# Attention values with the attention weights stationary, row sums from a ones column, and the result turned by the DMA crossbar

## Chip, cores, metric

One core of a Trainium2 chip. The metric is the time of one execution in device microseconds. The kernel before takes 1127.8 us (median of 4 runs, 1127.23 to 1130.22).

## The reference, cut to what matters

```python
def _attn_ref(q, kv, w_sr):            # q: 4 x 12288 x 128, kv: 4 x 384 x 32 x 128
    kv_pool = kv.reshape(B, H // 4, 4, W // 4, 4, C).mean(axis=(2, 4))
    k = v = kv_pool.reshape(B, -1, C) @ w_sr           # 768 keys of 128
    s = (q @ k.transpose(0, 2, 1)) / np.sqrt(C)
    a = softmax(s)                                      # rows of 768
    return a @ v

def _moe_ref(x, w_gate, w_val, w_out):                  # x: the 49152 attention rows; d_ff 1536
    return (np.maximum(x @ w_gate, 0) * (x @ w_val)) @ w_out
```

The kernel leaves the softmax unnormalised through the feed-forward part. Because that part is of degree two in x, one multiplication by the squared reciprocal of the row sum, at the very end, sets it right.

## The kernel before

A tile is 512 tokens, a group is four tiles, and there are 96 tiles. Tile k passes through a software pipeline: scores and exp in iteration k, values in k+1, value and gate projections in k+3, output projection in k+4. Cuts are marked with `# ...`.

```python
    def scores(k, jc):                       # TensorE, then exp on ScalarE
        s_ps = bank([128, T])
        nc.tensor.matmul(s_ps, kv16[:, k // NST, jc, 0, :], qT_of(k), start=True, stop=True)
        nc.scalar.activation(aTs[k][:, jc, :], s_ps, AF.Exp, scale=qk_scale)

    def values(k, jc):                       # kv stationary, 512 columns of weights stream
        # ...
        nc.tensor.matmul(xt_banks[k], kv16[:, k // NST, jc, 1, :], aTs[k][:, jc, :],
                         start=(jc == 0), stop=(jc == NJC - 1))
        if jc == NJC - 1:
            xTs[k] = work.tile([128, T], FP16, tag="xT", bufs=7, name="xT")
            nc.vector.tensor_copy(xTs[k], xt_banks.pop(k))       # already the way the next step wants it

    def row_sums(g):                         # once a group: 24 matmuls with a block of ones
        # ...
    def row_norms(g):                        # once a group: four fp32 transposes, reciprocal, square
        # ...

    def project(b, jc, pooled, copy_a, copy_b):       # pooled kv -> k and v
        tp = bank([128, 128])
        # ... transpose into tp
        kvT = work.tile([128, 128], FP32, tag="kvT")
        copy_a(kvT, tp)
        pr = bank([128, 2, 128])
        nc.tensor.matmul(pr[:, 0, :], w_sr_f32, kvT, start=True, stop=True)
        nc.tensor.matmul(pr[:, 1, :], kvT, w_sr_f32, start=True, stop=True)
        copy_b(kv16[:, b, jc], pr)
    # ... in the loop over k = 3 .. 98, for step in range(12):
    #     out_proj(k-4, step); value_proj(k-3, step); scores(k) or values(k-1); gate_proj(k-3, step)
    #     for each of batches 1 to 3, six times, in the batch before: kv_load (SyncE) at step 1,
    #     pooling on GpSimd at step 3 two tiles later, project at step 7 two tiles after that
```

The softmax here doesn't subtract the row's maximum and nothing guards it: scores larger than these inputs give would overflow.

## Time and profile before

| | before |
|---|---|
| time, median | 1127.8 us |
| span of the profiled run | 1125.7 us |
| TensorE, VectorE, ScalarE busy | 96%, 82%, 81% |
| one tile in the loop without inserts | 10.445 us |
| inserts per group (row sums, their turn) | 1.50 + 0.44 us |
| a tile with a kv projection (18 of them) | 11.27 us |

The rows on a tile and on inserts are distances from start to start. The lines are in the prediction.

### The profile page before, as it was taken

What the parts mean: (1) busy time and instruction counts of PE and PEld (TensorE: products, weight loads), DVE (VectorE), ACT (ScalarE), POOL (GpSimd) and SP (SyncE); (2) the same over time, 40 slices, a digit from 0 to 9 for tenths busy, and PEclk for the clock granted to TensorE, in tenths of its full rate; (3) what the DMA queues carried; (4) which work ended last, traced back from release to release, by engine and by line L of the source; (5) the groups of instructions that cost most, each with busy time, mean ns of one, the idle gap of its engine ahead of it and who ended that gap; (6) DMA issues with size and microseconds to landing.
All of it is one profiled execution on the core that took longest, in us unless ns stands there. A gap on an engine that the chain in (4) does not pass through costs nothing.

```text
span 1125.7 us, 23319 instructions
## 1 busy us (share of the span) xinstructions
PE 1077.6 (96%) x8874; PEld 636.3 (57%) x8874; DVE 920.1 (82%) x1470; ACT 909.2 (81%) x1741; POOL 119.8 (11%) x124
## 2 busy tenths in 40 slices
PE   0599999999999999999999999999999999999998
PEld 0245555556555555556555555555655555555555
DVE  1278888888888888888888888888888888888888
ACT  0488788778888888887888888878888888888886
POOL 1184000333000000042000000000000000000000
PEclk9999999999999999999999999999999999999999
DMA  9999530457303303313133033031230310201001
GB/s 217 222 220 245 94 57 30 94 118 156 66 24 62 58 29 66 57 30 57 35 52 65 22 66 58 29 58 47 39 67 23 64 38 29 48 20 29 20 29 38
DMA packets 166065, 78.24 MB, mean 70 GB/s; under 512 B 104129, under 2 KB 153409, under 8 KB 165953
## 3 DMA queue, kind: packets, MB, share of 16 engines
q1 hardware_dynamic: 112848, 59.85, 22.5%
q0 software_dynamic: 51376, 13.76, 12.1%
q10 hardware_dynamic: 1728, 3.15, 1.1%
q8 instruction: 69, 1.13, 0.4%
q14 instruction: 44, 0.35, 0.1%
HBM read 52.76 MB, written 25.17 MB: 69 GB/s over the span
## 4 chain that ended last, share of the span: by engine, by line
PE 94%; DMA 3%; ACT 1%; SPq 1%; DVE 0%; issue 0%; ACTq 0%; DVEq 0%; POOLq 0%
PE bank_ps L221 23%; PE bank_ps L196 22%; PE bank_ps L207 22%; PE bank_ps L150 11%; PE bank_ps L156 11%; PE bank_ps L170 3%; DMA q<-in_q_dram 1%; PE bank_ps L133 1%; PE bank_ps L182 1%; DMA parts<-in_kv_dram 1%; SPq L84 1%; DMA out_dram<-o_sb 1%; ACT aT L151 1%; PE bank_ps L134 1%; PE bank_ps L126 0%
## 5 line engine op out<-in xcount | busy, mean ns | idle before, releaser
L210 DVE SCALAR_TENSOR_TENSOR hT<-bank_ps,val 128x512 f16<-128x512 f32 x1152 | 764.7, 687 | 133.4 <-ACT val L200 83.2
L200 ACT CAST val<-bank_ps 128x512 f16<-128x512 f32 x1152 | 676.5, 589 | 166.1 <-PE bank_ps L196 164.6
L221 PEld LDWEIGHTS <-hT 128*128 128x128 f16 x4608 | 349.7, 98 | 262.9 <-issue 10.2
L221 PE MATMUL bank_ps<-wo,hT 128*128 128x128 f16 x4608 | 441.1, 219 | 0.9 <-DVE hT L210 0.8
L196 PE MATMUL bank_ps<-xT,wv 128*128 128x512 f16 x1152 | 436.6, 379 | 0.2
L207 PE MATMUL bank_ps<-xT,wg 128*128 128x512 f16 x1152 | 436.6, 379 | 0.0
L151 ACT ACTIVATE aT<-bank_ps 128x512 f16<-128x512 f32 x576 | 344.9, 602 | 3.1 <-PE bank_ps L150 3.1
L156 PE MATMUL bank_ps<-aT,kv 128*128 128x512 f16 x576 | 216.6, 379 | 2.8 <-DVE o_sb L229 2.1
L150 PE MATMUL bank_ps<-qT,kv 128*128 128x512 f16 x576 | 216.3, 381 | 2.4 <-ACT kv L138 2.4
L207 PEld LDWEIGHTS <-wg 128*128 128x128 f16 x1152 | 112.7, 98 | 134.5 <-issue 3.6
L196 PEld LDWEIGHTS <-wv 128*128 128x128 f16 x1152 | 112.7, 98 | 4.5 <-issue 1.4
L74 POOL DMA_DIRECT2D q<-in_q_dram x24 | 27.9, 1164 | 660.3 <-DMA qT<-q 659.5
L162 DVE CAST xT<-bank_ps 128x512 f16<-128x512 f32 x96 | 65.1, 680 | 10.7 <-PE bank_ps L156 10.7
L229 DVE TENSOR_TENSOR o_sb<-bank_ps,inv 128x512 f32<-128x512 f32 x96 | 65.3, 680 | 3.2 <-DMA out_dram<-o_sb 2.7
L150 PEld LDWEIGHTS <-kv 128*128 128x128 f16 x576 | 56.0, 98 | 6.2 <-ACT kv L138 4.0
L156 PEld LDWEIGHTS <-kv 128*128 128x128 f16 x576 | 56.3, 98 | 4.5 <-issue 1.2
L110 POOL TENSOR_TENSOR s<-parts 128x512 f32<-128x512 f32 x36 | 45.7, 1285 | 7.9 <-DMA parts<-in_kv_dram 7.1
L170 PE MATMUL bank_ps<-aT,ones 128*32 128x512 f16 x576 | 35.5, 381 | 0.0
L110 DVE TENSOR_TENSOR s<-parts 128x512 f32<-128x512 f32 x12 | 8.3, 692 | 33.2 <-DMA parts<-in_kv_dram 33.2
L133 PE MATMUL bank_ps<-kvT,w_sr_f 128*128 128x128 f32 x48 | 11.3, 319 | 24.5 <-ACT kvT L131 24.0
L131 ACT ACT_TABLE_LOAD x1 | 1.3, 1283 | 36.1 <-DMA parts<-in_kv_dram 36.1
L170 PEld LDWEIGHTS <-ones 128*32 128x32 f16 x576 | 13.2, 96 | 20.4 <-issue 9.9
(28 smaller groups left out, 161.5 us busy)
## 6 DMA issues: line engine op xcount, KB each, us to landing
out_dram<-o_sb SPq DMA_DIRECT2D x96, 256.0 KB, 2.2
parts<-in_kv_dram SPq DMA_DIRECT2D x84, 256.0 KB, 7.0
q<-in_q_dram POOLq DMA_DIRECT2D x24, 512.0 KB, 6.3
parts<-in_kv_dram ACTq DMA_DIRECT2D x12, 256.0 KB, 8.7
wv<-in_moe_w_val_dram POOLq DMA_DIRECT2D x1, 384.0 KB, 19.0
wg<-in_moe_w_gate_dram POOLq DMA_DIRECT2D x1, 384.0 KB, 21.2
wo<-in_moe_w_out_dram POOLq DMA_DIRECT2D x1, 384.0 KB, 25.5
qT<-q SPq DMA_TRANSPOSE x24, 4.3
```

Source lines behind the costliest of these rows:

```text
L110: eng.tensor_tensor(s2[:, i], parts[:, 2 * i], parts[:, 2 * i + 1], op=ALU.add)
L150: nc.tensor.matmul(s_ps, kv16[:, k // NST, jc, 0, :], qT_of(k), start=True, stop=True)
L151: nc.scalar.activation(aTs[k][:, jc, :], s_ps, AF.Exp, scale=qk_scale)
L156: nc.tensor.matmul(xt_banks[k], kv16[:, k // NST, jc, 1, :], aTs[k][:, jc, :], start=(jc == 0), stop=(jc == NJC - 1),)
L162: nc.vector.tensor_copy(xTs[k], xt_banks.pop(k))
L170: nc.tensor.matmul(r_ps[32 * i : 32 * i + 32, :], ones, aTs[g * GRP + i][:, jc, :], start=(jc == 0), stop=(jc == NJC - 1),)
L196: nc.tensor.matmul(va_ps, wv16[:, fb * 128 : (fb + 1) * 128], xTs[k], start=True, stop=True)
L200: nc.scalar.copy(val, va_ps)
L207: nc.tensor.matmul(g_ps, wg16[:, fb * 128 : (fb + 1) * 128], xTs[k], start=True, stop=True)
L210: nc.vector.scalar_tensor_tensor(hTs[k][:, fb, :], g_ps, 0.0, vals.pop((k, fb)), op0=ALU.max, op1=ALU.mult)
L221: nc.tensor.matmul(o_ps[:, s, :], hTs[k][:, fb, s * 128 : (s + 1) * 128], wo16[:, fb, :], start=(fb == 0 and s == 0), stop=(fb == NFB - 1) ...
L229: nc.vector.tensor_tensor(o_sb, o_banks.pop(k), inv2.to_broadcast([128, NS, 128]), op=ALU.mult)
```

## The change

The intent is to take the row sums off TensorE. With the attention weights stationary (128 tokens at a time) and k/v streaming, a column of ones beside v gives the row sum in the same matmul. The result then has tokens on the partitions and has to be turned before the projections, which a transposing DMA does (through the crossbar of the DMA engines). A second part of the change is the order of tokens: a q load now puts 16 consecutive tokens on a partition, four for each tile of the group, and an output write four.

```diff
-            q16, q[b, n0 : n0 + GRP * T, :].rearrange("(s p) c -> p s c", p=128)
+            q16, q[b, n0 : n0 + GRP * T, :].rearrange("(p s) c -> p s c", p=128)
-    kv16 = const.tile([128, B, NJC, 2, 128], FP16)
+    kv16 = const.tile([128, B, NJC, 2 * C + 4], FP16)          # k, v, ones
-    def values(k, jc):
-        nc.tensor.matmul(xt_banks[k], kv16[:, k // NST, jc, 1, :], aTs[k][:, jc, :], ...)
+    def values(k, jc, half):
+        for i in range(2):
+            s = 2 * half + i
+            nc.tensor.matmul(
+                x_ps[:, i, :], aTs[k][:, jc, s * 128 : (s + 1) * 128],
+                kv16[:, k // NST, jc, C : 2 * C + 1], ...)       # 129 columns
         if jc == NJC - 1:
-            nc.vector.tensor_copy(xTs[k], xt_banks.pop(k))
+            nc.vector.tensor_copy(x16s[k][:, own, :], x_ps[:, :, 0:C])
+            nc.vector.reciprocal(rinvs[k][:, own], x_ps[:, :, C])
+            if half == 1:
+                nc.sync.dma_start_transpose(xT, x16.rearrange("p s c -> p (s c)"))
+                nc.vector.tensor_tensor(inv2s[k][:, :, 0], rinv, rinv, op=ALU.mult)
-    def row_sums(g): ...
-    def row_norms(g): ...
-                out[k * T : (k + 1) * T, :].rearrange("(s p) c -> p s c", p=128), o_sb
+                out[k // GRP * GRP * T : (k // GRP + 1) * GRP * T, :].rearrange(
+                    "(p i s) c -> i p s c", p=128, i=GRP)[k % GRP], o_sb
     # ... before the loop: values of tiles 0 and 1 only (four before);
     #     tiles 2 and 3 follow in iterations 3 and 4; aT has 5 buffers (6 before)
```

More of the change, by code (lines that the diff above doesn't have):

```diff
@@ L134, in project @@
         nc.tensor.matmul(pr[:, 1, :], kvT, w_sr_f32, start=True, stop=True)
-        copy_b(kv16[:, b, jc], pr)
+        copy_b(kv16[:, b, jc, 0 : 2 * C], pr.rearrange("p i c -> p (i c)"))
     def act_scaled(dst, src):
@@ L141, in dve_scaled @@
         nc.vector.tensor_scalar(dst, src, 1.0 / (r * r), None, op0=ALU.mult)
-    aTs, xt_banks, xTs, hTs, o_banks, inv2s, vals = {}, {}, {}, {}, {}, {}, {}
+    aTs, x_banks, x16s, xTs, rinvs, inv2s = {}, {}, {}, {}, {}, {}
+    hTs, o_banks, vals = {}, {}, {}
     def scores(k, jc):
         if jc == 0:
-            aTs[k] = work.tile([128, NJC, T], FP16, tag="aT", bufs=6, name="aT")
+            aTs[k] = work.tile([128, NJC, T], FP16, tag="aT", bufs=5, name="aT")
         s_ps = bank([128, T])
-        nc.tensor.matmul(s_ps, kv16[:, k // NST, jc, 0, :], qT_of(k), start=True, stop=True)
+        nc.tensor.matmul(s_ps, kv16[:, k // NST, jc, 0:C], qT_of(k), start=True, stop=True)
@@ L151, in scores @@
         nc.scalar.activation(aTs[k][:, jc, :], s_ps, AF.Exp, scale=qk_scale)
-    def values(k, jc):
+    def values(k, jc, half):
         if jc == 0:
-            xt_banks[k] = bank([128, T])
-        nc.tensor.matmul(
-            xt_banks[k], kv16[:, k // NST, jc, 1, :], aTs[k][:, jc, :],
-            start=(jc == 0), stop=(jc == NJC - 1),
-        )
-        if jc == NJC - 1:
-            xTs[k] = work.tile([128, T], FP16, tag="xT", bufs=7, name="xT")
-            nc.vector.tensor_copy(xTs[k], xt_banks.pop(k))
@@ L164 @@
-    r_state = {}
-    def row_sums(g):
-        r_ps = bank([128, T])
-        for jc in range(NJC):
-            for i in range(GRP):
-                nc.tensor.matmul(
-                    r_ps[32 * i : 32 * i + 32, :], ones, aTs[g * GRP + i][:, jc, :],
-                    start=(jc == 0), stop=(jc == NJC - 1),
-                )
-        r_sb = work.tile([128, T], FP32, tag="r_sb")
-        nc.vector.tensor_copy(r_sb, r_ps)
-        r_state[g] = r_sb
-    def row_norms(g):
-        r_sb = r_state.pop(g)
-        rT = bank([128, NS, 128])
-        for s in range(NS):
-            nc.tensor.matmul(
-                rT[:, s, :], r_sb[:, s * 128 : (s + 1) * 128], ident,
-                is_transpose=True, start=True, stop=True,
-            )
-        rinv = work.tile([128, NS, GRP], FP32, tag="rinv")
-        nc.vector.reciprocal(
-            rinv, rT.rearrange("p s (g w) -> p s g w", g=GRP)[:, :, :, 0]
-        )
-        inv2 = work.tile([128, NS, GRP], FP32, tag="inv2", bufs=3)
-        nc.vector.tensor_tensor(inv2, rinv, rinv, op=ALU.mult)
-        inv2s[g] = inv2
+            x_banks[k, half] = bank([128, 2, C + 1])
@@ new lines, in values @@
+            if half == 0:
+                x16s[k] = work.tile([128, NS, C], FP16, tag="x16", bufs=3, name="x16")
+                rinvs[k] = work.tile([128, NS], FP32, tag="rinv", bufs=3, name="rinv")
+        x_ps = x_banks[k, half]
+        for i in range(2):
+            s = 2 * half + i
+            nc.tensor.matmul(
+                x_ps[:, i, :], aTs[k][:, jc, s * 128 : (s + 1) * 128],
+                kv16[:, k // NST, jc, C : 2 * C + 1],
+                start=(jc == 0 and i == 0), stop=(jc == NJC - 1), skip_group_check=True,
+            )
@@ new lines, in values @@
+        if jc == NJC - 1:
+            own = slice(2 * half, 2 * half + 2)
+            nc.vector.tensor_copy(x16s[k][:, own, :], x_ps[:, :, 0:C])
+            nc.vector.reciprocal(rinvs[k][:, own], x_ps[:, :, C])
+            if half == 1:
+                x16 = x16s.pop(k)
+                xT = work.tile([128, NS, 128], FP16, tag="xT", bufs=6, name="xT")
+                nc.sync.dma_start_transpose(xT, x16.rearrange("p s c -> p (s c)"))
+                xTs[k] = xT.rearrange("c s p -> c (s p)")
+                rinv = rinvs.pop(k)
+                inv2s[k] = work.tile([128, NS, 1], FP32, tag="inv2", bufs=6, name="inv2")
+                nc.vector.tensor_tensor(inv2s[k][:, :, 0], rinv, rinv, op=ALU.mult)
@@ L227, in out_proj @@
             o_sb = work.tile([128, NS, 128], FP32, tag="o_sb", bufs=3)
-            inv2 = inv2s[k // GRP][:, :, k % GRP : k % GRP + 1]
             nc.vector.tensor_tensor(
-                o_sb, o_banks.pop(k), inv2.to_broadcast([128, NS, 128]), op=ALU.mult
+                o_sb, o_banks.pop(k), inv2s.pop(k).to_broadcast([128, NS, 128]), op=ALU.mult
             )
             nc.sync.dma_start(
-                out[k * T : (k + 1) * T, :].rearrange("(s p) c -> p s c", p=128), o_sb
+                out[k // GRP * GRP * T : (k // GRP + 1) * GRP * T, :].rearrange(
+                    "(p i s) c -> i p s c", p=128, i=GRP
+                )[k % GRP], o_sb,
             )
@@ L244 @@
     make_identity(nc, ident)
-    ones = const.tile([128, 32], FP16)
-    nc.gpsimd.memset(ones, 1.0)
+    nc.gpsimd.memset(kv16[:, :, :, 2 * C : 2 * C + 4], 1.0)
     q_turn(0)
@@ L262 @@
         if jc > 0:
-            for k in range(LEAD):
-                values(k, jc - 1)
+            for k in range(2):
+                for half in range(2):
+                    values(k, jc - 1, half)
         if jc == 2:
@@ L268 @@
             nc.gpsimd.dma_start(wo16, moe_w_out.rearrange("(fb f) c -> f fb c", f=128))
-    for k in range(LEAD):
-        values(k, NJC - 1)
+    for k in range(2):
+        for half in range(2):
+            values(k, NJC - 1, half)
     q_turn(1)
@@ L292 @@
                     scores(k, step // 2)
-            elif LEAD <= k - 1 < NT:
-                values(k - 1, step // 2)
+            elif 2 <= k - 1 < NT:
+                half, i = divmod(step // 2, NJC // 2)
+                values(k - 1, 2 * i, half)
+                values(k - 1, 2 * i + 1, half)
             if 0 <= kF < NT:
                 gate_proj(kF, step)
-            if ph == 0 and k >= GRP and k // GRP <= NG:
-                if step == 2:
-                    row_sums(g - 1)
-                if step == 5:
-                    row_norms(g - 1)
             if b < B:
```

## The prediction

> **What bounds the kernel now.** I read the page's busy shares and its 40 slices first.
>
> ```profile
> PE 1077.6 (96%) x8874; PEld 636.3 (57%) x8874; DVE 920.1 (82%) x1470; ACT 909.2 (81%) x1741; POOL 119.8 (11%) x124
> PE   0599999999999999999999999999999999999998
> DMA  9999530457303303313133033031230310201001
> PE 94%; DMA 3%; ACT 1%; SPq 1%; DVE 0%; issue 0%; ACTq 0%; DVEq 0%; POOLq 0%
> ```
>
> TensorE is busy from slice 3 to the end, and 94% of the chain that ended last is TensorE. A busy TensorE is not proof, because matmuls overlap, so I then read the timeline of one stretch in the middle (TensorE only; columns are start us, length, line, count).
>
> ```profile
> 605.81 0.38 PE L207 MATMUL bank_ps<-xT,wg 128*128 128x512 f16 x1
> 606.03 0.39 PE L221 MATMUL bank_ps<-wo,hT 128*128 128x128 f16 x4
> 606.25 0.38 PE L196 MATMUL bank_ps<-xT,wv 128*128 128x512 f16 x1
> 606.47 0.38 PE L150 MATMUL bank_ps<-qT,kv 128*128 128x512 f16 x1
> 606.68 0.38 PE L207 MATMUL bank_ps<-xT,wg 128*128 128x512 f16 x1
> 606.99 1.48 PE L170 MATMUL bank_ps<-aT,ones 128*32 128x512 f16 x24
> 608.40 0.40 PE L221 MATMUL bank_ps<-wo,hT 128*128 128x128 f16 x4
> ...
> 610.81 0.38 PE L207 MATMUL bank_ps<-xT,wg 128*128 128x512 f16 x1
> 611.03 0.60 PE L182 MATMUL bank_ps<-ident,r_sb 128*128 128x128 f32 x4
> 611.47 0.39 PE L221 MATMUL bank_ps<-wo,hT 128*128 128x128 f16 x4
> ```
>
> The starts, not the lengths, are to be read: a 512-column matmul takes a slot of 0.216 us, four 128-column ones (each with its own weights) take 0.22 to 0.23, and no slot is empty. In the records' nanoseconds the median start-to-start is 216 ns for all 512-column lines and 56 ns for L221. So TensorE streams without a gap. A step of the loop (out 4x56, value 216, scores or values 216, gate 216) is 0.87 us, a tile of 12 steps 10.45 us (two output copies lie at 136.83 and 147.28), a group of four tiles 43.75 us. The group is 4 x 10.445 = 41.78 plus two inserts: the row sums (L170, 606.68 + 0.216 to 608.40: 1.50 us) and their turn (L182, 611.03 to 611.47: 0.44 us).
>
> **What the Trainium skill says.** "TensorE: Matmul & The Clock Gate", section "Wait — 56ns, not 53.3ns?", gives a warm start-to-start of N/2.4 + 2.5 ns: 55.6 for 128 columns and 215.7 for 512. The trace agrees (56 and 216). The same page, "Back-to-back issue gap", expects about 81 ns for a 128-column matmul with its own weight load; here L221 runs at 56 with a fresh load for each, so the loads (98 ns long in their rows, started 56 ns apart) are hidden and the trace decides. "DMA: Bandwidth & Descriptors", section "Specifications", asks for at least 512 B per descriptor for full rate; before, the q reads and out writes are runs of 512 B, so larger runs should help, and only where DMA is short. The same page's "Issuing engines are not separate DMA queues" says that all queues share the 16 engines; the early phase below shows it.
>
> **The change, part by part.** (1) Row sums and their turn go away: 24 x (1.50 + 0.44) = 46.6 us, all of it inserted in the gapless stream, so all on the path. (2) Values: 576 matmuls of 512 columns become 2304 of 129 columns, each with its own attention weights. Slot: 129/2.4 + 2.5 = 56.2 ns (an estimate from the page above and the 56 measured for 128). 576 x (4 x 56.2 - 216) = +5.1 us. The pattern "four short ones with loads between two long ones" is exactly that of L221, so I choose to believe that the loads stay hidden. (1)+(2): -41.5 us while TensorE is the bound.
>
> (3) VectorE. Per tile now: 12 gate products, one output copy, one xT copy and a quarter of the row-sum work. What counts is the start-to-start when it catches up:
>
> ```profile
> 604.41 0.68 DVE L229 TENSOR_TENSOR o_sb<-bank_ps,inv 128x512 f32<-128x512 f32 x1
> 605.01 0.68 DVE L162 CAST xT<-bank_ps 128x512 f16<-128x512 f32 x1
> 605.61 2.47 DVE L210 SCALAR_TENSOR_TENSOR hT<-bank_ps,val 128x512 f16<-128x512 f32 x4
> 612.13 0.25 DVE L187 RECIPROCAL rinv<-bank_ps 128x16 f32<-128x16 f32 x1
> 612.41 0.17 DVE L191 TENSOR_TENSOR inv<-rinv 128x16 f32<-128x16 f32 x1
> ```
>
> A full-bank operation costs 0.60, a tiny one 0.28 to 0.31. Removed per tile: 0.60 for xT and (0.60 + 0.28 + 0.31)/4 = 0.30. Added: two 128x256 copies at about 0.33 (half of 512 elements less the fixed part; an estimate), two reciprocals at 0.28, one product at 0.31: 1.53. VectorE goes from 12 x 0.60 + 0.60 + 0.90 = 8.7 to 9.3 us a tile, below TensorE's 10.45 + 0.05 = 10.50, so it stays beside the path, at 89%. Its page share should rise from 82% to about 88%. ScalarE has the same work: 909/1092 = 83%.
>
> (4) The xT turn moves to the DMA crossbar. Transposing 512 KB of q took 2048 packets of 256 B at 18 ns, 2.3 us of 16 engines; 128 KB is 0.58 us a tile, 55 us in all, on DMA that is idle two thirds of the time. From issue to landing q's took 4.3 us at best; a quarter of it perhaps 2.5 us (estimate). In the loop, tile k's values end in iteration k+1 and xT is wanted in k+3, so one iteration of 10.5 us covers it. (5) Four consecutive tokens: q's cast loads (51,376 packets in all, 41 ns each, 5.4 us of 16 engines per load) get longer runs, as do the out writes (0.87 us each). That is off the path except early.
>
> (6) The start is where I expect to pay. Until about 112 us DMA is full (9 in the first four slices), and the SyncE queue holds back whatever stands behind the kv loads:
>
> ```profile
> 60.93 11.10 SPq L101 DMA_DIRECT2D parts<-in_kv_dram  x11
> 72.78 7.94 SPq L84 DMA_TRANSPOSE qT<-q  x1
> 80.77 23.87 SPq L101 DMA_DIRECT2D parts<-in_kv_dram  x23
> 105.35 0.42 SPq L232 DMA_DIRECT2D out_dram<-o_sb  x1
> ```
>
> The first output was ready at 80.5 us and issued at 105.35, 25 us late; a q transpose takes 8 us to issue. Before, that cost one stall of 2.5 us (at 111.8, output buffers). Now xT itself goes through this queue. xT of tile 0 is ready to turn at about 62 us, where before it was used at once (61.5). I guess it is issued between 62 and 72 and lands 4 to 8 us after: TensorE waits 6 to 18 us, with 4 us of scores and values to fill in. Later tiles have an iteration of slack, and the delay itself gives them more. The old stall of 2.5 us should shrink. Two tiles' values move from the start into the loop (2.7 us), where the first gate products bound it anyway (12 x 0.60 = 7.2 us against 24 x 0.216 = 5.2). Net: +6 us, between 0 and +18.
>
> **Sum.** 1127.4 - 46.6 + 5.1 + 6 = 1092 us.
>
> **Rivals.** A: the weight loads from aT are not hidden, or an odd 129 columns costs extra. If a pair took the page's 81 ns: 2304 x 25 = +58 us, about 1150 and slower. Against it: L221 does the same at 56. For it: odd steps would then have 8 of 10 matmuls short. I give it 5%. B: VectorE or the PSUM banks become the bound. Its burst at a tile's end grows from 1.2 (output copy and xT) to about 1.5 us, plus 0.6 in the middle of the tile, with 0.27 us a step (0.87 less 0.60) to recover. The last copy and its reciprocals hold a bank while eight are near full. A gap of 0.1 us a tile is +10 us: about 1100. Before, the burst caused no TensorE gap, hence I count it as the upper part of the range. C: the SyncE queue holds xT for its whole 25 us lag, less a few us of slack: +20, so 1106 and only just 2%. D: nothing shows at the start, because the queue's order puts the transposes early and the longer q runs relieve DMA: 1083 to 1086.
>
> **Range and chances.** D and C set the ends: 1082 to 1107. The 2% line is 1104.8; only C with B, or A, crosses it. Faster 0.87, same 0.10, slower 0.03.
>
> **What would show it.** Right: L170 and L182 gone; the values line has 2304 matmuls 56 ns apart in start; group pitch about 42.0 us (4 x 10.50) instead of 43.75; VectorE near 88%; one TensorE wait on the xT transpose of 5 to 15 us between 60 and 75 us, and hardly any wait after 115; share of q0 down. Wrong: values starting over 60 ns apart (A); regular TensorE gaps that wait on VectorE (B); TensorE waits on xT in the middle of the run, which would mean that the transposes stand behind other work in the SyncE queue or take far longer than 2.5 us.

## More of the kernel before

Medians of several runs are quoted.

What the program writes is not the order that runs. A scheduler of the framework sorts each engine's instructions, and lets the kv loads of batches 1 and 2 run ahead from about 44 us on, although the program writes the first of them in iteration 12.

One more view is needed later, a projection of kv in the timeline of the kernel before (columns: start us, length us, engine, line, operation). First TensorE, then VectorE:

```profile
220.87 0.27 PE L126 MATMUL bank_ps<-ident,s 128*128 128x128 f32 x1
220.97 0.61 PE L221 MATMUL bank_ps<-wo,hT 128*128 128x128 f16 x8
221.61 0.46 PE L133 MATMUL bank_ps<-kvT,w_sr_f 128*128 128x128 f32 x2
```

```profile
221.18 0.29 DVE L131 COPY kvT<-bank_ps 128x128 f32<-128x128 f32 x1
```

The transpose of the pooled keys (L126, the last of it here) starts at 220.87, VectorE copies kvT at 221.18, and the projection matmul follows at 221.61: eight short output matmuls lie between, and they are enough.

## The result and the profile after

The changed kernel takes 1117.41 us (median of 4 runs, 1115.73 to 1119.26): ratio 0.9904, 95% interval 0.9881 to 0.9928. Ratios are the mean time of one kernel's runs over that of the other's of the same rounds, so they are not quite the ratios of the medians quoted. The change gains 1%, within the 2% line. The prediction was 1092 us, with 1082 to 1107 as its range.

From the page of the changed kernel: busy shares, slices of TensorE and of its granted clock, the chain by engine, then groups (busy us, mean ns | idle us before them) and a DMA issue with its us to landing.

```profile
PE 1041.0 (93%) x9930; PEld 688.4 (62%) x9930; DVE 918.9 (82%) x1782; ACT 904.8 (81%) x1741; POOL 104.3 (9%) x124
PE   0538999999999999999999999999999999999998
PEclk9969999999999999999999999999999999999999
PE 87%; DMA 6%; SPq 2%; ACT 2%; DVE 2%; issue 0%; POOL 0%; POOLq 0%; DVEq 0%
L185 PE MATMUL bank_ps<-xT,wv 128*128 128x512 f16 x1152 | 437.6, 380 | 25.7 <-DMA xT<-x 25.7
L165 PE MATMUL bank_ps<-kv,aT 128*128 128x129 f16 x2304 | 224.3, 220 | 0.1
xT<-x SPq DMA_TRANSPOSE x96, 2.5
```

The row sums are gone, and the chain has lost 7 points of TensorE to DMA, its queue, ScalarE and VectorE. The third slice of TensorE is down to 3 tenths, with the clock at 6 tenths there, and the value projection L185 waited 25.7 us in four places for xT. The 129-column matmuls themselves wait for nothing (0.1 us). Nor do the smaller buffers (aT has 5, before 6) show: after 115 us TensorE has no gap over 0.1 us but those named below and one of 0.8 us at the end, which the kernel before has too. Once in the loop, output copies are 10.515 us apart (134.79, 145.31 and on), against 10.445 before.

Where the waits lie is shown by the timeline of the changed kernel around the start, TensorE, then the SyncE queue (xN counts DMA issues, the length runs to the end of the last):

```profile
57.45 0.89 PE L165 MATMUL bank_ps<-kv,aT 128*128 128x129 f16 x8
76.87 0.58 PE L185 MATMUL bank_ps<-xT,wv 128*128 128x512 f16 x1 [18.53 <-DMA xT<-x]
...
79.39 0.63 PE L196 MATMUL bank_ps<-xT,wg 128*128 128x512 f16 x1
79.82 0.63 PE L185 MATMUL bank_ps<-xT,wv 128*128 128x512 f16 x1
```

```profile
50.83 16.24 SPq L103 DMA_DIRECT2D parts<-in_kv_dram  x17
67.65 6.62 SPq L85 DMA_TRANSPOSE qT<-q  x1
74.37 2.52 SPq L177 DMA_TRANSPOSE xT<-x  x2
```

VectorE has finished x of tile 0 at 58.6 us. Its transpose is issued at 74.37: for 16 us it stands behind kv loads, which themselves wait for pooling and for DMA, and then behind a q transpose that takes 6.6 us to issue. It lands 2.5 us after issue. TensorE stands still for 18.5 us, then works at half its clock (distance 0.43 us instead of 0.216): the nine slots from 76.87 to 80.64 take 3.8 us, which would be 2.0 at full clock. Two more gaps, of 3.3 and 3.4 us (start to start less the slot; the waits in them are 3.1 and 3.2 us), come near 96 and 110 us, and one of 1 us near 288.

The second loss is at the projections of kv. The changed kernel at one of them, TensorE, then VectorE:

```profile
236.81 0.27 PE L128 MATMUL bank_ps<-ident,s 128*128 128x128 f32 x1
236.92 0.61 PE L210 MATMUL bank_ps<-wo,hT 128*128 128x128 f16 x8
237.37 0.39 PE L165 MATMUL bank_ps<-kv,aT 128*128 128x129 f16 x4
237.60 0.44 PE L210 MATMUL bank_ps<-wo,hT 128*128 128x128 f16 x5
238.24 0.49 PE L135 MATMUL bank_ps<-kvT,w_sr_f 128*128 128x128 f32 x2 [0.20 <-DVE kvT L133]
```

```profile
237.30 0.69 DVE L199 SCALAR_TENSOR_TENSOR hT<-bank_ps,val 128x512 f16<-128x512 f32 x1 [0.29 <-ACT val L189]
237.91 0.28 DVE L133 COPY kvT<-bank_ps 128x128 f32<-128x128 f32 x1
238.99 0.42 DVE L143 TENSOR_SCALAR kv<-bank_ps 128x256 f16<-128x256 f32 x1 [0.80 <-PE bank_ps L136]
```

The kvT copy now stands behind one more gate product, which waits for ScalarE. It starts 1.1 us after the transpose (before: 0.3), and TensorE, with 17 short matmuls between, has run out of work. From the last output matmul to the projection the starts are 0.42 us apart instead of 0.056. VectorE in turn idles 0.8 us for the projection. A tile with a projection takes 11.68 us (before 11.27).

The spans add up, from the times of the output copies. To the end of tile 3: 114.32 before and 134.79 after, +20.5 us. That stretch held one group's inserts of 1.94 us before, so the start itself costs 22.4. From tile 3 to tile 91: -30.0, which is 22 x 1.94 us of inserts gone (-42.7), 88 x 0.07 of dearer values (+6.2), 18 x (11.68 - 0.07 - 11.27) = +6.1 at the projections and the one gap of 1 us: -29.4, within 0.6 us. The rest to the end, with the last insert, is -1.8. Together -11.3; the spans of the profiled runs are 1125.7 and 1114.4.

### The profile page after: what moved, and what is told of

Same layout as the page of the kernel before. It is cut to its first block, busy times and chain, and to the rows that moved or that the text cites. A ratio compares the mean times of both kernels' runs of the same rounds, so it can differ in the third digit from the quotient of the medians.

```text
span 1114.4 us, 26042 instructions
## 1 busy us (share of the span) xinstructions
PE 1041.0 (93%) x9930; PEld 688.4 (62%) x9930; DVE 918.9 (82%) x1782; ACT 904.8 (81%) x1741; POOL 104.3 (9%) x124
## 4 chain that ended last, share of the span: by engine, by line
PE 87%; DMA 6%; SPq 2%; ACT 2%; DVE 2%; issue 0%; POOL 0%; POOLq 0%; DVEq 0%
PE bank_ps L185 22%; PE bank_ps L196 22%; PE bank_ps L210 21%; PE bank_ps L165 11%; PE bank_ps L153 10%; DMA parts<-in_kv_dram 2%; DMA xT<-x 2%; SPq L85 2%; ACT val L189 2%; DMA qT<-q 2%; DVE hT L199 1%; PE bank_ps L135 1%; ACT aT L154 0%; SPq L103 0%; PE bank_ps L136 0%
## 5 line engine op out<-in xcount | busy, mean ns | idle before, releaser
L185 PE MATMUL bank_ps<-xT,wv 128*128 128x512 f16 x1152 | 437.6, 380 | 25.7 <-DMA xT<-x 25.7
L165 PE MATMUL bank_ps<-kv,aT 128*128 128x129 f16 x2304 | 224.3, 220 | 0.1
L165 PEld LDWEIGHTS <-aT 128*128 128x128 f16 x2304 | 177.1, 98 | 66.9 <-issue 1.1
L185 PEld LDWEIGHTS <-wv 128*128 128x128 f16 x1152 | 112.9, 98 | 13.0 <-DMA xT<-x 7.7
L172 DVE CAST x<-bank_ps 128x256 f16<-128x256 f32 x192 | 79.7, 415 | 9.8 <-PE bank_ps L165 9.8
L75 POOL DMA_DIRECT2D q<-in_q_dram x24 | 13.2, 549 | 675.0 <-DMA qT<-q 674.2
L153 PEld LDWEIGHTS <-kv 128*128 128x128 f16 x576 | 56.0, 98 | 8.2 <-ACT kv L140 4.1
L173 DVE RECIPROCAL rinv<-bank_ps 128x2 f32<-128x2 f32 x192 | 30.8, 160 | 0.0
L135 PEld LDWEIGHTS bank_ps<-kvT,w_sr_f 128*128 128x128 f32 x48 | 7.3, 193 | 30.5 <-ACT kvT L133 23.7
## 6 DMA issues: line engine op xcount, KB each, us to landing
wv<-in_moe_w_val_dram POOLq DMA_DIRECT2D x1, 384.0 KB, 12.1
```

The source lines that it names most:

```text
L153: nc.tensor.matmul(s_ps, kv16[:, k // NST, jc, 0:C], qT_of(k), start=True, stop=True)
L165: nc.tensor.matmul(x_ps[:, i, :], aTs[k][:, jc, s * 128 : (s + 1) * 128], kv16[:, k // NST, jc, C : 2 * C + 1], start=(jc == 0 and i == 0) ...
L172: nc.vector.tensor_copy(x16s[k][:, own, :], x_ps[:, :, 0:C])
L173: nc.vector.reciprocal(rinvs[k][:, own], x_ps[:, :, C])
L185: nc.tensor.matmul(va_ps, wv16[:, fb * 128 : (fb + 1) * 128], xTs[k], start=True, stop=True)
```

## The experiments

Three theories of the wait on xT were set against each other: Q, its place in the SyncE queue; D, full DMA engines; L, the mere length of the new way. For the projections, V and O, as the texts say. All eleven kernels give the right result.

**kv loads through another queue.**

```diff
-                    kv_load(b, at, [nc.sync])
+                    kv_load(b, at, [nc.gpsimd])
```

> The changed kernel with the kv loads of batches 1 to 3 issued from GpSimd instead of SyncE; the order of instructions on TensorE, VectorE and ScalarE is the same as in the changed kernel. Theory Q (the first xT transpose stands in the SyncE queue behind kv loads and a q transpose): with the kv loads out of that queue the 18.5 us TensorE wait on xT near 58 us falls to 4 to 9 us, the two waits of 3.3 us near 96 and 110 us vanish, and the time falls from 1117 to 1100 to 1108. Theory D (the 16 DMA engines are full, whoever issues): the same bytes still move, so the wait stays over 12 us and the time within 5 us of 1117. Theory L (copy, transpose and landing are simply that long): the wait stays at 18 us.

Measured: 1107.35 us (1105.92 to 1116.08), ratio 0.9831. TensorE and the SyncE queue of this kernel:

```profile
70.41 0.58 PE L185 MATMUL bank_ps<-xT,wv 128*128 128x512 f16 x1 [12.26 <-DMA xT<-x]
```

```profile
57.25 5.51 SPq L85 DMA_TRANSPOSE qT<-q  x1
62.86 18.59 SPq L177 DMA_TRANSPOSE xT<-x  x3
```

The time is where Q put it, the wait is not: it falls from 18.5 to 12.3 us, just over the 12 that D named. (The interval of the ratio, 0.979 to 0.9872, lies across the 2% line.) With no kv load in the queue, the transpose still stands behind a q transpose until 62.86. That is 11.5 us earlier than in the changed kernel, but it lands 7.5 us after issue, not 2.5; the share of the 16 DMA engines from 58 to 70.4 us is 1.12, in the changed kernel 1.06. So taking the kv loads out of the queue wins 6 us, and full engines, whoever feeds them, hold most of the rest. Two later waits on xT add 2.7 us.

**kv loads held back to their place in the program.** A copy of four columns of the current tile's attention weights into the load's buffer makes the load wait; the load then overwrites them.

```diff
     def kv_load(b, jc, engines, after=None):
         parts = work.tile([128, r, r, C], FP32, tag="kv_in", bufs=3)
+        if after is not None:
+            nc.gpsimd.tensor_copy(parts[:, :, 0, 0], after[:, 0, 0:r])
 ...
-                    kv_load(b, at, [nc.sync])
+                    kv_load(b, at, [nc.sync], after=aTs[k])
```

> The changed kernel with each kv load of batches 1 to 3 held back, by a tiny copy into its buffer from the attention weights of the tile in whose iteration the program writes the load, so that they no longer run ahead in the first 110 us. Theories Q and D both expect: TensorE wait on xT near 58 us of 3 to 6 us (0.6 copies, 1.2 issue, 2.5 landing, and perhaps a q transpose), no later ones, time 1093 to 1100. Theory L: wait stays near 18 us, time near 1117. If the wait falls here and not in the run with the other queue, it is the full engines; if it falls in both, it is the queue.

Measured: 1095.67 us (1094.35 to 1096.2), ratio 0.9713. The one wait left, on TensorE:

```profile
62.56 0.38 PE L187 MATMUL bank_ps<-xT,wv 128*128 128x512 f16 x1 [4.05 <-DMA xT<-x]
```

As Q and D had it, and L falls: the way itself is 4 us long. The wait fell in both runs, so neither of the two clean cases of the text came. Of the 18.5 us, 6 went with the queue alone, and another 8 only when the loads left the engines as well. No run frees the engines and leaves the queue full, so the split holds for this order of removal. The busy share of the 16 engines between 58 and 77 us is 0.42 here, against 1.05 in the changed kernel (it adds up the times of packets, so it can pass 1).

**The same hold in the kernel before, as a control.**

> Control: the kernel before with the same hold on the kv loads of batches 1 to 3. If holding the loads helps only because the change put xT into the SyncE queue, this gains no more than the one stall of 2.5 us and a little at the start: 1122 to 1127. If holding helps by itself (DMA freed for everything at the start), it gains 10 us or more: under 1118.

Measured: 1125.57 us, ratio 0.9982 (0.9957 to 1.0008). The run-ahead of the kv loads did the kernel before almost no harm. It is the change that made it matter.

**xT of the first two tiles by TensorE.**

```diff
+                if k < 2:                       # x kept in fp32 for these tiles
+                    for s in range(NS):
+                        nc.tensor.matmul(t_ps[:, s, :], x16[:, s, :], ident,
+                                         is_transpose=True, start=True, stop=True)
+                    nc.vector.tensor_copy(xT, t_ps)
+                else:
                     nc.sync.dma_start_transpose(xT, x16.rearrange("p s c -> p (s c)"))
```

> The changed kernel with xT of tiles 0 and 1 turned on TensorE (fp32, four 128x128 transposes each and one VectorE copy), all other tiles by the crossbar. Theory Q: the wait near 58 us goes, but the SyncE queue still reaches the transpose of tile 2 only near 90 us, so TensorE waits there instead: 8 to 14 us in all, time 1105 to 1112. Theory L (only the first transposes have no work to hide behind): waits in all under 7 us, time 1095 to 1100.

Measured: 1115.58 us (1110.78 to 1116.64), ratio 0.988: a wider spread than usual, and the median 3.6 us above what Q expected. The profiled run is the fastest of the four (1110.78). The wait moved, as Q said, to a later tile:

```profile
91.45 0.61 PE L197 MATMUL bank_ps<-xT,wv 128*128 128x512 f16 x1 [10.91 <-DMA xT<-x]
```

With two more, the waits on xT come to 14.4 us, where the changed kernel has 25.7. The span of this profiled run is 5.5 us shorter than that of the changed kernel, and the median 1.8 us lower; what uses up the rest of the 11 us was not taken apart. Helping the first tiles alone wins little, because tile 2 is then held in the same way. The queue issues its transpose at 84.75 us, after kv loads (93.51 in the changed kernel), and it lands 6.7 us later, while TensorE has nothing to do from 80.5 on.

**Projections two steps later.**

```diff
-                if step == 7 and 0 <= at - 4 < NJC:
+                if step == 9 and 0 <= at - 4 < NJC:
```

> The changed kernel with the 18 kv projections of batches 1 to 3 moved from step 7 to step 9 of the tile. Theory V (the copy of kvT comes late on VectorE because the first half of x is copied at step 5 and the gate products are still behind): the TensorE gaps of 0.42 and 0.32 us at each of the 18 projections shrink to under 0.15 us together, the tile with a projection falls from 11.68 to about 11.3 us, time -6 to -8 us. Theory O (it is only how the instructions happen to be ordered around a projection, in any step): gaps of the same size, time within 2 us of the changed kernel.

Measured: 1118.63 us, ratio 0.9915. Waits on kvT of TensorE grew from 3.6 to 10.3 us in total, and the tile took 11.88. V, in the form that the copy of the first half of x at step 5 is to blame, is out. O has the time but not the gaps, which it expected to keep their size. What stands between the transpose and its use remains, and the next two runs test that.

**kvT copied by ScalarE, on top of the hold.**

```diff
-    project(b, at - 4, kv_s3.pop((b, at - 4)), nc.vector.tensor_copy, dve_scaled)
+    project(b, at - 4, kv_s3.pop((b, at - 4)), nc.scalar.copy, dve_scaled)
```

> The held kernel with only the kvT copy of the 18 projections moved from VectorE to ScalarE, everything else at its step. If the wait at the projection comes from kvT's place in VectorE's queue, it goes or falls to under 0.15 us each: time -4 to -8, 1088 to 1092. If it comes from how few matmuls TensorE has between transpose and projection, it stays: within 2 us of 1095.7.

Measured: 1090.44 us, ratio 0.9666; a tile with a projection takes 11.40 us instead of 11.68. So kvT's place in VectorE's queue is worth 18 x 0.28 = 5.0 us, which is what the medians lose (5.2). The copy now starts 0.32 us after the transpose, as in the kernel before, but only six short matmuls lie between transpose and projection, and the tile still takes 0.33 us more than its work.

**The projection split over two steps, on top of the hold.**

```diff
                 if step == 7 and 0 <= at - 4 < NJC:
-                    project(b, at - 4, kv_s3.pop((b, at - 4)), nc.vector.tensor_copy, dve_scaled)
+                    kvTs = project(b, at - 4, kv_s3.pop((b, at - 4)), nc.vector.tensor_copy, None)
+                if step == 9 and 0 <= at - 4 < NJC:
+                    project_end(b, at - 4, kvTs, dve_scaled)
```

> The held kernel (1095.7) with each kv projection of batches 1 to 3 split: transpose and kvT copy at step 7, the two projection matmuls at step 9, so that the copy has two steps to come. Theory O (at each projection TensorE waits on the kvT copy, which stands behind a gate product in VectorE's queue): the 0.42 us gaps go, a tile with a projection falls from 11.68 to 11.25 to 11.35 us, time -6 to -8: 1088 to 1090. If instead VectorE is simply short of time in those tiles, the gap comes back elsewhere and the time stays within 2 us of 1095.7.

Measured: 1085.59 us (1083.09 to 1086.64), ratio 0.9616. More than expected: a tile with a projection takes 11.07 us, the 10.515 of a tile and 0.555 for the transpose (0.11) and the four projection matmuls (0.22 for each two). TensorE in this kernel, from the transpose to the projection:

```profile
226.16 0.27 PE L130 MATMUL bank_ps<-ident,s 128*128 128x128 f32 x1
...
227.81 0.38 PE L203 MATMUL bank_ps<-xT,wg 128*128 128x512 f16 x1
228.02 0.38 PE L142 MATMUL bank_ps<-kvT,w_sr_f 128*128 128x128 f32 x2
```

Two steps now lie between, and no slot is empty. The split also removes what the kernel before lost there, which the expectation had left out.

**Both, and the values of tiles 2 and 3 ahead of the loop.**

```diff
+    for k in range(2, LEAD):
+        for half in range(2):
+            for jc in range(NJC):
+                values(k, jc, half)
 ...
-            elif 2 <= k - 1 < NT:
+            elif LEAD <= k - 1 < NT:
```

> As the run before, and the values of tiles 2 and 3 put ahead of the loop, where TensorE has nothing to do but wait for xT of tile 0. The wait of 4.3 us near 58 us falls to about 1.5 us and the clock isn't lowered after it: another -2 to -4 us, 1085 to 1088. This would be the best version.

Measured: 1081.27 us (1079.82 to 1082.03), ratio 0.9579. TensorE in this kernel:

```profile
58.26 3.38 PE L172 MATMUL bank_ps<-kv,aT 128*128 128x129 f16 x56
63.28 0.38 PE L192 MATMUL bank_ps<-xT,wv 128*128 128x512 f16 x1 [1.64 <-DMA xT<-x]
63.50 0.38 PE L203 MATMUL bank_ps<-xT,wg 128*128 128x512 f16 x1
```

The wait is filled with value matmuls, and the matmuls after it are 0.22 us apart at once, at full clock. This version beats both kernels.

**Hold and split in the kernel before, as a control.**

> Control: the kernel before with both the held loads and the split projection. The tiles with a projection take 11.27 us there against 10.445 plus 0.555 of projection matmuls, so the split should gain 18 x 0.27 = 5 us over the held kernel before (1125.6): 1119 to 1122. The changed kernel with both (1085.6) is then 34 to 36 us faster: what the change itself is worth in TensorE time, against the 41.5 predicted less what its start costs.

Measured: 1120.54 us, ratio 0.9934. Against 1085.59 for the changed kernel with the same two repairs, the change is worth 35 us by the medians and 39 by the spans of the profiled runs (1120.7 and 1081.3), which are the slowest of the one kernel and the fastest of the other. By the parts it should be 41.5 as predicted, less 1.6 for dearer values and 2.0 for what is left of the start (tile 3 ends at 113.68 against 113.58, where the kernel before has 1.94 us of inserts to do): 37.9.

**The token order alone**, in the kernel before (two lines of the diff), and the changed kernel with the old order.

> The kernel before with only the token part of the change: four consecutive tokens to a partition in the q loads and the output writes. Prediction's part 5: off the path except early, so at most the one stall of 2.5 us shrinks: 1122 to 1129, and the time that q0's packets took falls from 12.1% to about 7%. If the output writes or q loads had been holding TensorE unseen, it gains over 5 us.

Measured: 1124.72 us (1122.62 to 1129.38), ratio 0.9974. The share of q0 fell from 12.1% to 7.1%, as expected, and the time hardly.

> The changed kernel with the old token order (128 tokens apart) in the q loads and output writes. If the longer runs relieve the full DMA engines at the start, this is slower than the changed kernel, with the TensorE wait on xT near 58 us longer than 18.5 us by 2 to 8 us: 1119 to 1125. If the token order doesn't matter, within 2 us of 1117.

Measured: 1124.34 us, ratio 0.996, so 7 us slower than the changed kernel. The longest wait on xT is 21.1 us instead of 18.5, and TensorE comes to it 4.7 us later (63.1 against 58.3 us); from tile 3 to tile 91 the two kernels agree within 0.7 us. The token order does matter there, through the crowded start only. Without it the change would have gained 0.4%.

## Why the prediction was wrong

1. *Row sums and their turn, -46.6 us on the path.* Right: in the stretch between tiles 3 and 91, where the loop runs, 22 of 24 groups gave 1.94 us each, and the sum closes within 0.6 us.
2. *Values, +5.1 us.* Right in kind, a little small: 0.07 us a tile, not 0.053, so 6.7 us. The loads stay hidden and the starts are 57 ns apart by the median. Rival A is out.
3. *VectorE stays beside the path.* Right in the loop, for a partly wrong reason. Its share stayed at 82% where 88% was predicted, because a 128x2 reciprocal delays the next, independent instruction by 0.08 us (58.12 to 58.20 in the timeline), not by the 0.28 read off a pair of which one needed the other, and the product of 0.31 likewise takes 0.07. The added work is 0.88 us a tile, not 1.53, against 0.90 removed. Rival B, a gap in every tile, is out.
4. *The turn takes 2.5 us and one iteration covers it.* Right in the loop: 2.5 us to landing, and after 115 us a single wait on xT, of 1 us, in 90 tiles.
5. *Longer runs help only early.* Right, and there worth 7 us in the changed kernel (after_old_tokens). The page's 512 bytes do not say so, since runs of 512 bytes, as the prediction counts the old ones, meet them already; the experiment does.
6. *The start: net +6 us, between 0 and +18.* This is the step that failed, by size. It measured +22.4. The queue and the full engines were both named, and "issued between 62 and 72" missed by only 2 us (74.37). But x was ready at 58.6, not 62, and the wait of 18.5 us lies just over the top of the 6 to 18 forecast. What was set against it did not come: the "4 us of scores and values to fill in" did not run ahead. Between 58.3 and 76.87 us no matmul starts, because the value projection that needs xT stands before them in TensorE's order; in the last of the repaired kernels (hold_split_fill), where values stand first, they do fill the time. The "iteration of slack" of later tiles didn't suffice either (waits of 3.1 and 3.2 us), and the pause lowered the clock, for 1.8 us more. These four make 26.6; the old stall of 2.2 us is gone, and the last 2 us or so, with two tiles' values moved behind the wait, were not taken apart. Rival C had the size nearly right (+20), in part by luck: it had the queue hold xT for 25 us, where it held it for 16 and the later waits and the clock made up the rest. It was given too little weight, and its 1106 us lies over the 2% line of 1104.8 by itself, although the prediction says that only C with B, or A, crosses it.
7. *What was left out.* No step asked what the change does to the other work that depends on the order around it. The 18 projections lost 6.1 us more, because kvT's copy came to stand behind a gate product. In the run with ScalarE and the one with the split, the cause showed: 5 us for the place of the copy, 5 more by the medians (18 x 0.33 = 5.9 by the tiles) for the few matmuls in between, part of which the kernel before lost as well.

The sum from 1092 to 1117: 16.4 us of the start, 6.1 of the projections, 1.6 of the values and the 1 us gap make 1117. Why the scheduler put kvT's copy behind that gate product in the changed kernel was not tried; that VectorE has more instructions to place is likely, not shown.

The clock's fall agrees in kind with the Trainium skill, "TensorE: Matmul & The Clock Gate", section 'The HAM clock gate (the "warmup" mystery)', which gives half rate after an idle window of about 3.4 us and until about 3.4 us of work: here 427 ns for 512 columns until 80.3 us, 3.4 us after work resumed. The times agree only roughly. The trace records the fall at 60.1 us, 1.8 us after the last matmul ended; in the other runs where a wait lowered the clock, the record has the fall 1.7 to 5.1 us after TensorE stopped and the rise 3.2 to 6.0 us after it went on. The waits of 3.1 and 3.2 us in the changed kernel didn't lower it.

## What to carry to other kernels

When a change puts a transfer into the path that used to be a copy, ask of the queue it goes through what stands ahead of it at the worst moment, in time and not only in bytes: a lag that was harmless for outputs becomes a stall of the engine that sets the end. Prefetches that run far ahead are not free; hold them to when they are wanted. And give every value that crosses two engines a step or two of other work between production and use, because a small shift of order elsewhere uses up a tight gap.

## What the Trainium skill lacked or had wrong

- "TensorE: Matmul & The Clock Gate", section "Back-to-back issue gap", gives about 81 ns for a sustained pair of weight load and 128-column matmul. Both kernels run 4608 such pairs at 56 ns, and the changed one 2304 of 129 columns at 57 ns. For 512 columns it gives about 131 ns; here the median is 216.
- "DMA: Bandwidth & Descriptors", section "DMA Transpose (X-bar)", itself has no figure for what a transpose costs the queue that issues it (the page has cycle counts for this only in a table on trn3 B0 against "previous generations"). Here 128 KB took 1.2 us to issue and 2.5 us to land on idle engines, 512 KB 1.9 and 4.3 us, and on full engines, in the first 75 us of both kernels, 512 KB took 6 to 12 us to issue, with all behind it waiting.
- The same page, "Issuing engines are not separate DMA queues", says that several queues only save the time to issue, usually small beside the transfer. Here moving the kv loads to another queue took 6 us off a wait of 18.5: a queue also holds back what stands behind an instruction that waits. In the changed kernel it held xT for 16 us.
